# Pooling attention and a routed MLP on one core: 128-token chunks as two 64-column tiles, two attention accumulators, four shared PSUM banks, and half as many comparisons per score

## The chip, the cores and the metric

One core of a Trainium2 chip runs the whole program. The metric is the device time of one execution in microseconds (us), lower is better. The engines of the core are named as in the profile: PE (TensorE, with its weight loads listed apart as PEld), DVE (VectorE), ACT (ScalarE), POOL (GpSimd) and SP (SyncE, which here only issues DMAs).

## The reference

Inputs q, k and v have the shape (8 batches, 8 heads, 576 tokens, 64), all float32. Keys and values are averaged over groups of 8 tokens, so each head has 72 of each.

```python
k_p = k.reshape(B, H, Sp, pool, D).mean(axis=3)
v_p = v.reshape(B, H, Sp, pool, D).mean(axis=3)
scores = scale * np.matmul(q, k_p.transpose(0, 1, 3, 2))
attn = np.exp(scores - max); attn = attn / (np.sum(attn) + 1e-09)
x = np.matmul(attn, v_p)                     # (B, S, H*D) after a transpose
scores = np.einsum('bsd,d->bs', x, w_gate)   # one number per token
top_idx = np.argpartition(-scores[b], capacity)[:capacity]    # 128 of 576
h = np.maximum(x[b, top_idx] @ w1, 0.0)      # 512 -> 1024
out[b, top_idx] = x[b, top_idx] + sigmoid(scores[b, top_idx])[:, None] * (h @ w2)
```

All other rows of `out` are `x`.

## The kernel before

`direct_path` computes the softmax without subtracting the maximum and writes a flag if a sum of exponentials left a safe range; `general_path`, which the change does not touch, would then compute everything again. With these inputs it is not entered.

Attention goes by units and chunks. A batch has 3 units of 192 tokens (`u`) and 6 chunks of 96 tokens (`a`). `q_trans` (L204, DVE) transposes the queries of a unit. `scores` (L209 to L222) makes its scores with 16 float32 matmuls on four row tiles of 32 rows (two heads to a tile pair; 72 key columns as weights, 192 queries streamed), all into `pS`, four PSUM banks with one buffer, and one ACT instruction (L220) takes the exponential of all 1536 columns into `et`, where it writes with a stride. `attend` (L226) runs, per chunk, 8 matmuls, one per head: 96 columns of `et` are the weights, and 66 columns of pooled values `vp` are streamed: 64 values, a column of 8s for the sum, a column of the gate product. The result `pA` is two banks with one buffer. `norm` (L236) reads it: ACT copies the sums (L244, adding eps) and the gate sums (L245), DVE takes the reciprocal (L247) and multiplies (L248) into `xs`. Every float32 matmul appears as two records in the trace, a transpose by a matmul as one.

Pooling adds up raw rows on POOL: `pool_k` (L169, L170) and twice `pool_v` (L186 to L190) per batch, and DVE rearranges the keys (`k_trans`, L175, L179) and reduces the gate product (`gate_v`, L194).

The routed MLP of a batch follows its attention. `score` sums the gate column, `row_bcast` spreads all 576 scores along the free axis (6 transposes, two ACT copies), and `count` compares every score with every other: per chunk one comparison "at least" with the chunks ahead (L305), one "greater" with its own and those behind (L307), and one for ties (L309). `one_hot` and `gather` make a list of 128 rows, an indirect DMA on POOL's queue reads them back from `out` (L331), `x_trans` transposes them, `hidden` runs 8 blocks of 4 matmuls (128 columns each), `finish` 8 matmuls of 512 columns into `pF`, one DVE instruction (L373) adds the residual, and a second indirect DMA (L374) scatters the rows.

Each engine executes in program order, and that order is written out by hand in the loop over `a` (L440 to L452): jobs of slot 0, `attend` and `norm` of chunk `a`, slot 1, `scores` of the next unit (after even `a`) and `q_trans` of the one after it, slots 2 and 3. `at` puts the jobs into slots: the MLP of batch b starts `hidden` at chunk 6(b+1)+8, 14 chunks after the first chunk of the batch, one block per slot, in between the attention of later batches. Loads are issued from SP two batches ahead (the first values and all stores of `xs` from ACT's queue). PSUM is full: 4 banks `pS`, 2 `pA`, 1 `pM` (all small MLP products), 1 `pF`.

Of the kernel before, what the change touches and what calls it, by code (L numbers as in the profile page):

```python
# [7 lines left out]
FT = mybir.dt.float32  # L8
# [40 lines left out]
def direct_path(ctx, tc, q, k, v, moe_w_gate, moe_w1, moe_w2, moe_capacity, out, flag):  # L49
# [7 lines left out]

    nc = tc.nc
# [6 lines left out]
    C = 96  # L65
    NC = S // C
    CT = C // G
    NTH = NC // 2
    N3 = 2 * C
# [8 lines left out]
    assert 2 <= cap <= 128 and DM == 512 and D == 64 and H == 8 and S == 576 and F == 1024  # L78
    NU = B * NTH
    NCH = B * NC  # L80
# [5 lines left out]
    psum = ctx.enter_context(tc.tile_pool(name="psum", bufs=1, space=bass.MemoryType.PSUM))  # L86
# [14 lines left out]
    def load_v(b, g, eng):  # L101
        x = work.tile([SP, HG, POOLW, D], FT, name="vraw", bufs=3)
        VR[b, g] = x
        src = v[b, HG * g : HG * (g + 1)].rearrange("h (p t) d -> p h (t d)", t=POOLW)
        for lo, hi in ((0, 64), (64, SP)):
            eng.dma_start(out=x[lo:hi].rearrange("p h t d -> p h (t d)"), in_=src[lo:hi])

    load_k(0)
    load_v(0, 0, nc.scalar)
    load_q(0)  # L110
    load_v(0, 1, nc.scalar)
# [3 lines left out]
    wg = const.tile([SP, H, D], FT)  # L115
    nc.scalar.dma_start(out=wg.rearrange("p h d -> p (h d)"),
                        in_=bass.AP(tensor=moe_w_gate.tensor, offset=moe_w_gate.offset, ap=[[0, SP], [1, DM]]))
    eps = const.tile([C, 1], FT)
    nc.vector.memset(eps, 1e-9 * POOLW)
    diff = const.tile([128, 128], FT)  # L120
    nc.gpsimd.iota(diff, pattern=[[1, 128]], base=0, channel_multiplier=-1,
                   allow_small_or_imprecise_dtypes=True)
    slots = const.tile([C, cap], FT)
    nc.gpsimd.iota(slots, pattern=[[1, cap]], base=0, channel_multiplier=0,
                   allow_small_or_imprecise_dtypes=True)
    part = const.tile([C, 1], FT)
    nc.gpsimd.iota(part, pattern=[[0, 1]], base=0, channel_multiplier=1, allow_small_or_imprecise_dtypes=True)
    chunk0 = const.tile([C, NC], FT)
    nc.gpsimd.iota(chunk0, pattern=[[1, NC]], base=0, channel_multiplier=0, allow_small_or_imprecise_dtypes=True)
    vps = []  # L130
    for i in range(2):
        t = const.tile([SP, H, E], FT, name=f"vp{i}")
        nc.gpsimd.memset(t[:, :, D : D + 1], float(POOLW))
        vps.append(t)
    ident = const.tile([128, 128], FT)
    before = const.tile([C, C], FT)
    ones = const.tile([C, 1], FT)
    zall = const.tile([C, B, NC, H], FT)
    cmp = const.tile([C, S], BF)
# [4 lines left out]
    def constants():  # L144
        nc.vector.tensor_scalar(ident, diff, 0.0, None, op0=OP.is_equal)
        nc.vector.tensor_scalar(before, diff[:C, :C], 0.0, None, op0=OP.is_lt)
        nc.vector.memset(ones, 1.0)

        hi = const.tile([C, 1], FT, name="hi")
        stepped = const.tile([C, CT], FT, name="stepped")  # L150
        for t in range(CT):
            nc.vector.tensor_scalar(stepped[:, t : t + 1], part, float(G * (t + 1)), None, op0=OP.is_ge)
        nc.vector.tensor_reduce(out=hi, in_=stepped, axis=AX.X, op=OP.add)
        lo = const.tile([C, 1], FT, name="lo")
        nc.vector.scalar_tensor_tensor(lo, hi, -float(G), part, op0=OP.mult, op1=OP.add)
        nc.vector.tensor_scalar(lo, lo, float(NC), None, op0=OP.mult)
        nc.vector.tensor_scalar(hi, hi, float(NC * G), None, op0=OP.mult)
        for a in auxb:
            nc.vector.tensor_scalar(a[:, :, 0], chunk0, lo, None, op0=OP.add)
            nc.vector.tensor_scalar(a[:, :, 1], chunk0, 0.0, hi, op0=OP.mult, op1=OP.add)  # L160
# [11 lines left out]
    def k_trans(b):  # L172
# [4 lines left out]
        KT[b] = work.tile([128, 2, 2, SP], FT, name="kt")  # L177
        x = half.rearrange("p j c r -> p (j c r)").rearrange("p (n two) -> p n two", two=2)
        nc.vector.tensor_tensor(out=KT[b].rearrange("p j s n -> p (j s n)"), in0=x[:, :, 0], in1=x[:, :, 1],  # L179
                                op=OP.add)  # L180
# [17 lines left out]
    QT, ET, XS, SS, RZ = {}, {}, {}, {}, {}  # L198

    def q_trans(u):  # L200

        b, th = divmod(u, NTH)
        QT[u] = work.tile([128, 2, 2, CT, 32], FT, name="qt")
        nc.vector.transpose(  # L204
            out=QT[u].rearrange("p cc j t c -> p t (cc j) c"),
            in_=QR[b].rearrange("p (t c) d -> p t (c d)", c=NC)[:, :, 2 * D * th : 2 * D * (th + 1)].rearrange(
                "p t (a e) -> p t a e", e=32))

    def scores(u):  # L209
        b = u // NTH  # L210
        p = psum.tile([SP, 4, 4, 128], FT, name="pS")
        for s in range(2):
            for j in range(2):
                for i in range(4):
                    r = slice(32 * i, 32 * i + 32)
                    nc.tensor.matmul(p[:, i, 2 * s : 2 * s + 2, 0:C], KT[b][r, j, s, :],  # L216
                                     QT[u][r, :, j, :, G * s : G * s + G],
                                     start=(j == 0), stop=(j == 1))
# [601 lines left out]
```

## Time and profile before

| | |
|---|---|
| three runs | 365.93 us median (361.97 to 368.25) |
| the profiled execution | 366.8 us, of which the span of the trace is 364.9 us |
| busy share of the span | PE 75%, PEld 59%, DVE 49%, POOL 37%, ACT 29% |
| chain that ended last, by engine | PE 44%, DVE 22%, DMA 16%, ACT 6%, issue 5%, POOL 4% |
| mean granted clock of TensorE | 0.865 of full speed |

The profiled execution is a single one, 0.9 us above the median. The chain of work that ended last is followed back from the last instruction through whatever released each step; a line's share of it is the time it set, unlike its busy time. Busy time of PE is modelled by the profiler and records overlap, so a count of records times the distance at which blocks follow each other is a better price than the length of one record. The level of TensorE's clock is 1.2 or 2.4 GHz; a granted clock in between is a mean over a stretch.

### The profile page before, as it was taken

How to read it: one execution, taken by the hardware profiler on the slowest of the kernel's cores; microseconds unless marked ns; L12 is line 12 of the kernel's file. 1: busy time of each engine (PE TensorE's matmuls, PEld its weight loads, DVE VectorE, ACT ScalarE, POOL GpSimd, SP SyncE). 2: the span in 40 equal slices, each digit the busy share in tenths (PEclk: the TensorE clock that was granted, in tenths of full speed). 3: DMA queues.
4: the chain of work that ended last, by engine and by line, in shares of the span. 5: the costliest groups of instructions: out<-in, count | busy, mean ns of one | idle time of the engine just before them, and what ended most of it. 6: DMA issues, size and time to landing. Idle time of an engine off the chain costs nothing.

```text
span 364.9 us, 5869 instructions
## 1 busy us (share of the span) xinstructions
PE 275.2 (75%) x2306; PEld 216.3 (59%) x2306; DVE 177.9 (49%) x524; ACT 104.9 (29%) x169; POOL 134.5 (37%) x156
## 2 busy tenths in 40 slices
PE   0303777788658988969778989698879889989890
PEld 0203666576637875767557755686668669556650
DVE  3249244158423752594429723946294627563001
ACT  0310333422240444324314441432343244110100
POOL 1177501950359015660647064805390210121101
PEclk9999766655565998988999998969996999999996
DMA  7932999961781178306661686031121113210101
GB/s 272 268 58 54 372 353 304 321 140 44 208 249 50 44 195 247 94 15 151 224 158 31 141 295 142 0 110 46 38 65 43 46 29 93 66 60 11 48 0 39
DMA packets 12952, 46.75 MB, mean 128 GB/s; under 512 B 1324, under 2 KB 1324, under 8 KB 10868
## 3 DMA queue, kind: packets, MB, share of 16 engines
q1 hardware_dynamic: 8240, 31.33, 29.4%
q10 hardware_dynamic: 3396, 10.77, 10.0%
q0 software_dynamic: 1280, 4.20, 4.2%
q8 instruction: 20, 0.33, 0.4%
q14 instruction: 16, 0.13, 0.1%
HBM read 34.75 MB, written 11.53 MB: 127 GB/s over the span
## 4 chain that ended last, share of the span: by engine, by line
PE 44%; DVE 22%; DMA 16%; ACT 6%; issue 5%; POOL 4%; ACTq 1%; DVEq 0%; SPq 0%; POOLq 0%
PE pA L232 14%; PE pM L358 10%; PE pS L216 8%; DMA xr<-out_dram,idx 8%; PE pF L368 8%; DMA vraw<-in_v_dram 7%; DVE xs L248 4%; ACT et L220 4%; DVE cmp L309 3%; POOL kraw L169 2%; DVE cmp L305 2%; DVE qt L204 2%; DVE cmp L307 2%; DVE oh L316 2%; DVE kh L175 2%
## 5 line engine op out<-in xcount | busy, mean ns | idle before, releaser
L232 PE MATMUL pA<-vp,et 72*96 72x66 f32 x768 | 90.8, 281 | 47.7 <-DVE vp L194 24.6
L232 PEld LDWEIGHTS pA<-vp,et 72*96 72x96 f32 x768 | 86.3, 195 | 59.0 <-issue 28.5
L220 ACT ACTIVATE et<-pS 72x1536 f32<-72x1536 f32 x24 | 70.7, 2947 | 61.9 <-PE pS L216 61.9
L358 PE MATMUL pM<-xg,w 128*128 128x128 f32 x512 | 71.3, 292 | 2.8 <-ACT xg L348 1.5
L358 PEld LDWEIGHTS pM<-xg,w 128*128 128x128 f32 x512 | 65.0, 203 | 8.7 <-issue 5.0
L368 PE MATMUL pF<-w,ht 128*128 128x512 f32 x128 | 65.2, 632 | 0.0
L247 DVE RECIPROCAL rz<-zall 96x8 f32<-96x8 f32 x48 | 9.5, 198 | 113.9 <-ACT zall L244 112.4
L216 PE MATMUL pS<-qt,kt 32*72 32x192 f32 x768 | 52.4, 428 | 12.0 <-DVE qt L204 12.0
L216 PEld LDWEIGHTS pS<-qt,kt 32*72 32x72 f32 x768 | 36.5, 184 | 19.4 <-DVE qt L204 12.0
L281 POOL CAST auxb<-sc 96x6 bf16<-96x6 f32 x8 | 1.6, 199 | 121.0 <-DVE sc L277 105.0
L186 POOL TENSOR_TENSOR vraw<-vraw 72x1024 f32<-72x1024 f32 x15 | 35.5, 2368 | 19.7 <-DMA vraw<-in_v_dram 19.6
L244 ACT ACTIVATE zall<-pA,eps 96x8 f32<-96x8 f32 x48 | 12.2, 254 | 93.8 <-PE pA L232 93.8
L248 DVE TENSOR_TENSOR xs<-pA,rz 96x512 f32<-96x512 f32 x48 | 33.0, 687 | 6.7 <-DVE rz L247 0.9
L368 PEld LDWEIGHTS pF<-w,ht 128*128 128x128 f32 x128 | 22.9, 200 | 17.9 <-issue 17.9
L307 DVE TENSOR_SCALAR_CACHE_REDUCE cmp<-sr,sc 96x576 bf16<-96x576 f32 (+5 forms) x48 | 26.6, 554 | 0.0
L204 DVE STREAM_TRANSPOSE qt<-qraw 128x768 f32<-128x768 f32 x24 | 23.2, 966 | 0.9 <-DMA qraw<-in_q_dram 0.9
L374 POOL DMA_INDIRECT out_dram<-y,idx x8 | 8.5, 1064 | 40.1 <-DVE y L373 22.0
L309 DVE SCALAR_TENSOR_TENSOR cmp<-sr,sc,before 96x96 bf16<-96x96 f32 x48 | 21.9, 456 | 0.3
L373 DVE SCALAR_TENSOR_TENSOR y<-pF,g,xr 128x512 f32<-128x512 f32 x8 | 6.0, 750 | 29.5 <-PE pF L368 29.5
L305 DVE TENSOR_SCALAR_CACHE_REDUCE cmp<-sr,sc 96x96 bf16<-96x96 f32 (+4 forms) x40 | 20.0, 499 | 0.7
L187 POOL TENSOR_TENSOR vraw<-vraw 72x512 f32<-72x512 f32 x15 | 19.1, 1277 | 1.2
L361 ACT ACTIVATE ht<-pM 128x512 f32<-128x512 f32 x16 | 9.6, 597 | 33.6 <-PE pM L358 33.6
(68 smaller groups left out, 182.4 us busy)
## 6 DMA issues: line engine op xcount, KB each, us to landing
kraw<-in_k_dram SPq DMA_DIRECT2D x8, 1152.0 KB
qraw<-in_q_dram SPq DMA_DIRECT2D x8, 1152.0 KB, 6.7
out_dram<-xs ACTq DMA_DIRECT2D x24, 384.0 KB, 3.0
vraw<-in_v_dram SPq DMA_DIRECT2D x14, 512.0 KB, 9.0
w<-in_moe_w_dram SPq DMA_DIRECT2D x2, 2048.0 KB, 27.3
vraw<-in_v_dram ACTq DMA_DIRECT2D x2, 512.0 KB, 19.9
vraw<-in_v_dram SPq DMA_DIRECT2D x14, 64.0 KB
wg<-in_moe_w_gate_dram ACTq DMA_DIRECT2D x1, 144.0 KB
```

Of the source, the lines that this page charges most:

```text
L186: eng.tensor_tensor(out=x[:, :, 0:4, :], in0=x[:, :, 0:4, :], in1=x[:, :, 4:8, :], op=OP.add)
L187: eng.tensor_tensor(out=x[:, :, 0:2, :], in0=x[:, :, 0:2, :], in1=x[:, :, 2:4, :], op=OP.add)
L204: nc.vector.transpose(out=QT[u].rearrange("p cc j t c -> p t (cc j) c"), in_=QR[b].rearrange("p (t c) d -> p t (c d)", c=NC)[:, :, 2 * D * ...
L216: nc.tensor.matmul(p[:, i, 2 * s : 2 * s + 2, 0:C], KT[b][r, j, s, :], QT[u][r, :, j, :, G * s : G * s + G], start=(j == 0), stop=(j == 1))
L220: nc.scalar.activation(ET[u].rearrange("p n g t -> p n t g"), p.rearrange("p i n x -> p (i n) x")[:, :, 0:C].rearrange("p n (t g) -> p n t ...
L232: nc.tensor.matmul(p[:, g, E * n : E * n + E], ET[u][:, 2 * h + cc].rearrange("p g t -> p (g t)"), VP[b][:, h, :], start=True, stop=True)
L248: nc.vector.tensor_tensor(out=XS[b][:, c, :].rearrange("p (g n d) -> p g n d", g=2, d=D), in0=o[:, :, :, 0:D], in1=rz.rearrange("p (g n on ...
L305: nc.vector.tensor_scalar(cmp[:, 0 : c * C], row[:, 0 : c * C], s, None, op0=OP.is_ge, op1=OP.add, accum_out=CN[b][:, c, 0:1])
L307: nc.vector.tensor_scalar(cmp[:, c * C : S], row[:, c * C : S], s, None, op0=OP.is_gt, op1=OP.add, accum_out=CN[b][:, c, 1:2])
L309: nc.vector.scalar_tensor_tensor(cmp[:, 0:C], row[:, c * C : c * C + C], s, before, op0=OP.is_equal, op1=OP.mult, accum_out=CN[b][:, c, 2:3])
L358: nc.tensor.matmul(p[:, f % 4, :], w1[:, d, 128 * f : 128 * f + 128], XG[b][:, d, :], start=(d == 0), stop=(d == DB - 1))
L368: nc.tensor.matmul(p, HT[b][:, f, :], w2[:, f, :], start=(f == 0), stop=(f == FB - 1))
```

## The change

Tokens are taken in tiles of 64 (`TL`), 9 to a batch; a unit is three tiles (still 192 tokens), and a chunk two tiles, 128 tokens, so that two batches share 9 chunks. In `attend` each of the 8 heads has two matmuls with 64 weight columns each; one writes PSUM partitions 0 to 63, the other 64 to 127 of the same bank. `pA` gets two buffers. The four banks that scores use are now single tiles `bank0` to `bank3`, which all MLP products share; each bank has its own exponential, and `et` is written densely. Pooled values and keys are spread over 128 partitions with zeros between (an extra one carries eps), so score matmuls have 128 weight columns. `norm` leaves ACT: DVE takes the reciprocal from PSUM and forms the gate score.

`count` makes one "at least" comparison per chunk, with the chunks up to its own, times a mask, with the sum along the row; `one_hot` gets the other half of each count as 15 matmuls of the comparison matrices with a column of ones. `hidden` runs in parts of 3, 3 and 2 blocks, `finish` in three column slices (176, 176, 160), each scaled on ACT and added on POOL. Stores and all loads of values move to SP's queue. Value loads get four fixed buffers. The slots are rearranged: `hidden` of batch b starts in unit 3(b+1)+3, and scores run two units ahead at the start, one later.

```diff
+    vraws = [const.tile([128, HG, POOLW, D], FT, name=f"vraw{i}") for i in range(4)]
+    for i, t in enumerate(vraws):
+        (nc.vector, nc.gpsimd)[i % 2].memset(t, 0.0)
...
+        nc.sync.dma_start(out=x[0:128:2], in_=src[0:64])
+        nc.sync.dma_start(out=x[1:128:16], in_=src[64:SP])
...
+    first = const.tile([C, 1], FT)
+    nc.vector.memset(first, 1.0)
+    nc.scalar.activation(first, first, AF.Exp)
...
+        nc.vector.tensor_reduce(out=y[:, :, 0:128:2], in_=x[:, :, 0:64, :], axis=AX.X, op=OP.add)
+        nc.vector.tensor_reduce(out=y[:, :, 1:128:16], in_=x[:, :, 64:SP, :], axis=AX.X, op=OP.add)
...
+        for s in tiles_of(b, th):
+            x = QR[b][:, s, :].rearrange("p t (j e) -> p t j e", e=32)
+            m = x.shape[1]
+            nc.vector.transpose(out=QT[u][:, :, n : n + m, :].rearrange("p j t c -> p t j c"), in_=x)
...
+        p = [bank(i, [128, 2, TS * TL]) for i in range(4)]
...
+                    nc.tensor.matmul(p[i][:, s, :], KT[b][r, j, s, :], QT[u][r, j, :, G * s : G * s + G],
                                      start=(j == 0), stop=(j == 1))
+        ET[u] = [work.tile([128, 2, TS * TL], FT, name=f"et{i}", bufs=3) for i in range(4)]
+        for i in range(4):
+            nc.scalar.activation(ET[u][i], p[i], AF.Exp, scale=exp_scale)
...
+        PA[a] = psum.tile([C, 2, 512], FT, name="pA")
...
+            for t in range(2):
+                u, i = divmod(2 * a + t, TS)
+                nc.tensor.matmul(PA[a][TL * t : TL * t + TL, g, E * n : E * n + E],
+                                 ET[u][h // 2][:, h % 2, TL * i : TL * i + TL], VP[u // NTH][:, h, :],
+                                 start=True, stop=True)
...
+        nc.vector.reciprocal(rz, o[:, :, :, D])
...
+        nc.vector.tensor_tensor(out=SS[a // NT][:, a % NT, :].rearrange("p (g n) -> p g n", g=2),
+                                in0=o[:, :, :, D + 1], in1=rz, op=OP.mult)
...
+        for i, cs in enumerate((range(0, NC - 1), range(NC - 1, NC))):
+            p = bank(i, [C, len(cs), C])
...
+        for c in range(NC):
+            nc.vector.scalar_tensor_tensor(GE[b][c], SR[b][:, 0 : c + 1, :], scs[b % 2][:, c : c + 1],
+                                           before[:, NC - 1 - c : NC, :], op0=OP.is_ge, op1=OP.mult,
+                                           accum_out=CN[b][:, c : c + 1])
...
+        p = bank(2, [C, NC])
+        for c in range(NC):
+            for i in range(c, NC):
+                nc.tensor.matmul(p[:, c : c + 1], GE[b][i][:, c, :], ones, start=(i == c), stop=(i == NC - 1))
...
+        fs = range(FB)[3 * part : 3 * part + 3]
+        p = bank(nb, [128, len(fs), cap])
...
+        c = slice(176 * part, min(176 * part + 176, DM))
+        p = bank(nb, [cap, c.stop - c.start])
+        for f in range(FB):
+            nc.tensor.matmul(p, HT[b][:, f, :], w2[:, f, c], start=(f == 0), stop=(f == FB - 1))
+        nc.scalar.activation(Y[b][:, c], p, AF.Copy, scale=g)
+        nc.gpsimd.tensor_tensor(out=Y[b][:, c], in0=Y[b][:, c], in1=XR[b][:, c], op=OP.add)
...
+        for n, f in enumerate((row_bcast, count, one_hot, gather, gate, x_trans)):
+            du, slot = ((0, 1), (0, 2), (0, 6), (1, 4), (1, 6), (2, 5))[n] if b == B - 1 else (
+                (0, 3), (0, 7), (1, 3), (1, 7), (2, 2), (2, 7))[n]
+            at(w + du, slot, f, b)
+        at(w + 3, 3, hidden, b, 0, 0)
+        at(w + 3, 5, hidden, b, 1, 1)
+        at(w + 4, 3, hidden, b, 2, 0)
+        at(w + 4, 5, finish, b, 0, 1)
+        at(w + 5, 5, finish, b, 1, 2)
+        at(w + 5, 6, finish, b, 2, 3)
...
+            at(u, 1, pool_k, b + 1, nc.gpsimd)
+            at(u, 7, pool_v, b + 1, 0, nc.gpsimd)
+            at(u + 1, 3, k_trans, b + 1)
+            at(u + 1, 7, pool_v, b + 1, 1, nc.gpsimd)
...
+    load_k(1)
+    load_v(1, 0)
+    load_v(1, 1)
+    load_q(1)
...
+    constants()
     pool_k(0, nc.vector)
     pool_v(0, 0, nc.gpsimd)
     k_trans(0)
     q_trans(0)
     scores(0)
+    q_trans(1)
+    scores(1)
+    eights()
+    gate_v(0, 0)
     pool_v(0, 1, nc.vector)
     gate_v(0, 1)
...
+    for u in range(NU + 6):
+        run(u, 0)
+        mine = chunks.get(u, ())
+        for a in mine[0:1]:
+            attend(a)
+            norm(a)
+        run(u, 1)
+        if 0 < u < NU - 1:
             scores(u + 1)
+        run(u, 2)
+        for a in mine[1:]:
+            attend(a)
+            norm(a)
+        if u + 2 < NU:
+            q_trans(u + 2)
+        for slot in range(3, 8):
+            run(u, slot)
```

A unit `u` has one chunk when it is even and two when it is odd; `w` is 3(b+1).

## Rows read from the trace of the kernel before

**Rows 1.** The page's first part: busy time and instructions of each engine.
```profile
PE 275.2 (75%) x2306; PEld 216.3 (59%) x2306; DVE 177.9 (49%) x524; ACT 104.9 (29%) x169; POOL 134.5 (37%) x156
```
**Rows 2.** Chain of waits, 30 to 63 us: start us, us, what. One unit.
```profile
42.48 2.83 PE pA L232 x16
45.30 2.82 PE pS L216 x32
...
48.21 2.93 ACT et L220
...
51.52 0.70 DVE xs L248
...
52.27 2.83 PE pA L232 x16
```
**Rows 3.** Stretches: from:to, us, busy us (records) PE, PEld, DVE, ACT, POOL, granted clock, DMA.
```profile
33.00:111.00 78.00, 55.73 (x466) 46.89 (x467) 34.41 (x105) 25.05 (x40) 30.53 (x34) 0.64 0.79 240
111.00:148.60 37.60, 34.86 (x288) 27.20 (x289) 19.05 (x62) 13.01 (x21) 14.08 (x17) 0.84 0.48 134
...
261.60:298.80 37.20, 32.42 (x292) 25.94 (x290) 21.56 (x63) 13.03 (x21) 13.78 (x17) 0.91 0.16 47
```
**Rows 4.** Chain of waits, 111 to 365 us: blocks of records, in order of time.
```profile
120.65 1.33 PE pA L232 x16
121.98 1.84 PE pM L358 x16
...
126.10 1.47 PE pS L216 x32
127.57 1.09 PE pM L358 x8
...
180.97 7.21 DMA xr<-out_dram,idx
...
316.35 0.30 PE pM L323 x6
...
319.26 0.45 PE pM L293 x3
...
322.39 0.64 PE pM L346 x4
...
349.69 6.03 PE pF L368 x14
355.74 0.75 DVE y L373
```
**Rows 5.** Timeline of PEld, 301 to 303 us: the weight loads of one unit's scores.
```profile
301.29 1.19 PEld L216 LDWEIGHTS pS<-qt,kt 32*72 32x72 f32 x32
```
**Rows 6.** Groups by line and shape: operation, shapes, count, busy us, mean ns, idle before.
```profile
L232 PE MATMUL pA<-vp,et 72*96 72x66 f32 x768 | 90.8, 281 | 47.7 <-DVE vp L194 24.6 <-DVE xs L248 20.6 <-DVE ss L275 2.5
L186 POOL TENSOR_TENSOR vraw<-vraw 72x1024 f32<-72x1024 f32 x15 | 35.5, 2368 | 19.7 <-DMA vraw<-in_v_dram 19.6
L361 ACT ACTIVATE ht<-pM 128x512 f32<-128x512 f32 x16 | 9.6, 597 | 33.6 <-PE pM L358 33.6
L295 ACT COPY sr<-pM 96x288 f32<-96x288 f32 x16 | 6.7, 418 | 8.0 <-PE pM L293 8.0
```
**Rows 7.** Timeline, 148 to 189 us: POOL and DVE side by side, then DVE's instruction again.
```profile
155.63 2.34 POOL L186 TENSOR_TENSOR vraw<-vraw 72x1024 f32<-72x1024 f32 x1
...
155.98 2.11 DVE L309 SCALAR_TENSOR_TENSOR cmp<-sr,sc,before 96x96 bf16<-96x96 f32 x1
...
161.15 0.31 DVE L309 SCALAR_TENSOR_TENSOR cmp<-sr,sc,before 96x96 bf16<-96x96 f32 x1
```
**Rows 8.** Timeline, 0 to 36 us: the start.
```profile
2.27 31.39 SPq L106 DMA_DIRECT2D vraw<-in_v_dram  x4
...
16.72 2.35 POOL L186 TENSOR_TENSOR vraw<-vraw 72x1024 f32<-72x1024 f32 x1 [15.17 <-DMA vraw<-in_v_dram]
...
32.96 2.80 PE L232 MATMUL pA<-vp,et 72*96 72x66 f32 x16 [18.09 <-DVE vp L194]
```

More of the change, by code (lines that the diff above doesn't have):

```diff
@@ L123, in direct_path @@
[L123 to L134, printed above, removed]
@@ new lines, in direct_path @@
+    vps = [const.tile([128, H, E], FT, name=f"vp{i}") for i in range(2)]
+    kts = [const.tile([128, 2, 2, 128], FT, name=f"kt{i}") for i in range(2)]
+    for t in kts + vps:
+        nc.gpsimd.memset(t, 0.0)
+    slots = counted("slots", [C, NC, cap], [[C, NC], [1, cap]], 1 - NC * C, 1)
+    before = const.tile([C, NC, C], FT)
+    nc.gpsimd.memset(before[:, 0 : NC - 1, :], 1.0)
+    scs = [const.tile([C, NC], FT, name=f"sc{i}") for i in range(2)]
+    nc.gpsimd.memset(scs[0][TL:C, NC - 1 : NC], -3e38)
@@ L145, in constants @@
         nc.vector.tensor_scalar(ident, diff, 0.0, None, op0=OP.is_equal)
-        nc.vector.tensor_scalar(before, diff[:C, :C], 0.0, None, op0=OP.is_lt)
+        nc.vector.tensor_scalar(before[:, NC - 1, :], diff, 0.0, None, op0=OP.is_lt)
         nc.vector.memset(ones, 1.0)
[L149 to L160, printed above, removed]
+        nc.vector.memset(one32, 1.0)
@@ L256, in direct_path @@
+    SR, CN, GE, OH, XR, GV, XG, HT, Y = ({} for _ in range(9))
     store, scat, gath = {}, {}, {}
@@ L319, in gather @@
     def gather(b):
-        p = psum.tile([cap, 5], FT, name="pM")
+        p = bank(2, [cap, 5])
         for c in range(NC):
@@ L343, in x_trans @@
     def x_trans(b):
-        p = psum.tile([128, DB, cap], FT, name="pM")
+        p = bank(0, [128, DB, cap])
         for d in range(DB):
@@ L348, in x_trans, with hidden @@
         nc.scalar.copy(out=XG[b], in_=p)
-    def hidden(b, f):
-        if f == 0:
+    def hidden(b, part, nb):
+        if part == 0:
             HT[b] = work.tile([128, FB, cap], FT, name="ht")
-        if f % 4 == 0:
-            PH[b] = psum.tile([128, 4, cap], FT, name="pM")
-        p = PH[b]
-        for d in range(DB):
-            nc.tensor.matmul(p[:, f % 4, :], w1[:, d, 128 * f : 128 * f + 128], XG[b][:, d, :],
-                             start=(d == 0), stop=(d == DB - 1))
-        if f % 4 == 3:
-            nc.scalar.activation(HT[b][:, f - 3 : f + 1, :], p, AF.Relu)
@@ new lines, in hidden, with finish @@
+        p = bank(nb, [128, len(fs), cap])
+        for n, f in enumerate(fs):
+            for d in range(DB):
+                nc.tensor.matmul(p[:, n, :], w1[:, d, 128 * f : 128 * f + 128], XG[b][:, d, :],
+                                 start=(d == 0), stop=(d == DB - 1))
+        nc.scalar.activation(HT[b][:, fs[0] : fs[-1] + 1, :], p, AF.Relu)
+    def finish(b, part, nb):
+        idx, g = GV[b]
+        if part == 0:
+            Y[b] = work.tile([cap, DM], FT, name="y")
+        c = slice(176 * part, min(176 * part + 176, DM))
[4 more added lines that the diff above has]
+        nc.gpsimd.tensor_tensor(out=Y[b][:, c], in0=Y[b][:, c], in1=XR[b][:, c], op=OP.add)
+        if part == 2:
+            i = nc.gpsimd.indirect_dma_start(
+                out=out_rows, out_offset=bass.IndirectOffsetOnAxis(ap=idx[:, :1], axis=0), in_=Y[b], in_offset=None)
+            others(i, b, (store, scat, gath))
+            scat[b] = [i]
```

321 lines of the change are left out of this document (150 added, 171 removed).

## Prediction

> **What bounds the kernel now.** I read the busy shares first. TensorE is the busiest engine, at 75% of the span [rows 1], but an average over stages settles nothing, so the stretches come next. Three stages show: nothing but attention until 111 us, then five batches in which attention and MLP interleave, then two MLPs alone.
>
> In the first stage TensorE is busy 55.73 of 78 us, at a mean granted clock of 0.64 [rows 3]. The chain of waits says why that is no TensorE bound: a unit goes round in 9.79 us (42.48 to 52.27), as attend 2.83, scores 2.82, exponential 2.93, division 0.70 [rows 2]. Two properties make it a ring. `pA` has one buffer, so the next attend waits for the division; and the division's inputs come from ACT, which in program order first does the exponential of the next unit. Blocks here last twice as long as later: attend 2.83 against 1.33, scores 2.82 against 1.47 [rows 2, 4]. That is the lower of the two clock levels.
>
> In the middle stage five batches take 187.8 us (111.0 to 298.8), 37.6 each, of which TensorE is busy 32.42 in the last, at a granted clock of 0.91 [rows 3]. Block distances at the high level give its bare work per batch: attend 6 x 1.33 = 8.0; scores 3 x 1.47 = 4.4; hidden, 64 records at 1.84/16 = 0.115, 7.4; finish, 16 at 6.03/14 = 0.43, 6.9; 6 broadcasts at 0.15, 6 small products at 0.05 and 4 transposes at 0.16, 1.8 [rows 4]. The sum is 28.5, so 9.1 us per batch are waits and low clock. The ring of the first stage still exists here, and the read-back of the gathered rows takes 7.21 us [rows 4].
>
> **The change, part by part.**
>
> *Attend.* A chunk of 128 tokens has 32 records instead of 16, and a batch 4.5 chunks instead of 6. No row shows column tiles, so both bounds are worked out. Hidden streams 128 columns and loads 128 in 0.115 us per record, attend loads 96 and streams 66 in 0.083 [rows 4]: 0.9 ns per column, whichever of the two is longer, the other hidden. With 64 loaded and 66 streamed a record costs 0.059. If the two tiles go one after the other, a chunk takes 32 x 0.059 = 1.88 us; if side by side, 0.94. The nearest row is scores, which run four row tiles: 32 records of 192 streamed columns would take 5.5 us in turn and take 1.47 [rows 4], 0.11 above a quarter. I take side by side with that surcharge, 1.05 us per chunk, 4.7 per batch, and keep 8.5 as the other end.
>
> *Scores.* The streamed columns stay, the loaded ones grow from 72 to 128. All 32 loads now lie within 1.19 us [rows 5]; in proportion 2.1, if they are the limit, 1.47 if not. I take 1.6, since the loads overlap across row tiles; 4.8 per batch.
>
> *Mode changes.* Attend becomes a tiled block between scores (row tiles) and MLP (none). Where the trace has such a change, the 8 records of hidden behind scores take 1.09 instead of 0.92 [rows 4]: 0.17. Per batch there are 10.5 changes instead of 6; at 0.17 that is 0.8 more. Here a rule speaks against the change: the Trainium skill, TensorEngine Tiling (Array Packing), Key Properties, says that changing the tiling mode drains the engine, while changing the tile within a mode does not. If such a drain cost a whole record's 0.28 us [rows 6] each time, the sum would grow by 1.3 instead of 0.8 per batch, 3 us over the kernel; the trace's 0.17 is what I use.
>
> *MLP.* Hidden stays 7.4. Finish loads its weights three times as often, but 176 columns streamed at 0.9 ns still cover 128 loaded: 48 records, 7.4. Broadcasts, 5 at 0.16, 0.8. Column sums are new: 15 small products like gather's, 0.05 each [rows 4], 0.75. Gather and transposes 0.9. With attend, scores and mode changes TensorE's bare work is 27.5 us per batch.
>
> *ACT* loses the sums and copies of `norm`, and the stores' issue. Rows of 512 and 288 dense columns, 0.597 and 0.418 [rows 6], give 0.19 plus 0.8 ns per column, so an exponential of 384 costs 0.5, four 2.0, instead of 2.93. TensorE hides all of it: scores are a unit ahead. Without cover it would be 2 us per unit.
>
> *DVE* gets one small product more per chunk but counts in five instructions instead of 17. Rows of 96 and 512 columns, 0.31 and 0.75 [rows 4, 7], give 0.2 plus 1.06 ns per column: 128 to 640 columns, 3.1 us plus five reads of the sum. DVE was busy 21.56 us in a batch [rows 3]; at or below that it lies under TensorE's 27.5. `q_trans` and `k_trans` in two pieces cost some tenths and hide there too. POOL has 134.5/8 = 16.8 us per batch [rows 1] and gets three additions, 176 columns at 2.368/1024 each [rows 6], 1.2 more: hidden.
>
> *Counting under POOL.* A masked comparison of 96 columns took 2.11 us while POOL ran a pooling step, and 0.31 alone [rows 7]. The new count is five such instructions with two inputs, and a batch's first `pool_v` is queued right behind it. The least extra is nothing; the most is one POOL step before each, about the 4.7 us of one `pool_v` (2048 columns at 2.3 ns). The Trainium skill, SBUF — State Buffer, Who interferes with whom, has it so: two inputs from SBUF contend with POOL reading SBUF, one input does not. If by that rule the whole 4.7 fell on each count with no cover, the sum would be 6 x 3.7 = 22 us longer, near rival 2. The row bears it out in kind, not in how often. Between count and the column sums, TensorE has hidden, attend and scores of some 7 us to do, so I charge 1 us of wait.
>
> *Waits that remain,* per batch: the broadcast now shares a bank with hidden and waits for its Relu (0.6 [rows 6]), the next hidden part waits for the broadcast's copy (0.9), count 1, read-back 1. Together 3.5. The ring of [rows 2] is gone: with two `pA` buffers an attend waits for the division of the chunk before last. A batch then takes 27.5 + 3.5 = 31 us against 37.6.
>
> *Queue of SP.* Stores wait there for `xs`, with the loads of two batches later behind them. In the old start SP is held 31.39 us by value loads that wait for a buffer [rows 8]; four buffers end that. A store waits at most a unit, and loads have two batches: nothing is charged.
>
> *Start.* Values are ready for POOL at 16.72, the first attend runs at 32.96 [rows 8]. In the new order POOL pools one half (4.7), DVE reduces it (0.4), pools the other (2048 columns at 1.06, 2.2) and reduces that: 25 us; 33 if POOL holds DVE up as before.
>
> *First two batches,* six units. POOL's pooling, 5824 columns per batch at 2.3 ns, is 4.5 us per unit; TensorE needs 1.5 x 1.05 + 1.6 = 3.2 at the high clock level and 6.4 at the low one. I take 5.7, bounds 4.5 and the old 9.79. That is 34 us.
>
> *Tail* after the last unit: two hidden and two finish 29.6, broadcast, sums, gather, transposes 2.4, two Relus and copies 1.2, a wait for read-back 3, and from the last finish to the span's end 364.9 - 355.7 = 9.2 [rows 4] plus some tenths: 46.
>
> *Sum:* 25 + 34 + 6 x 31 + 46 = 291, plus the 1.9 us that the profiled execution has outside its span (366.8 - 364.9): 293. That execution lies 0.9 above the median of the runs, which I neglect.
>
> **The rivals.**
>
> 1. *Tiles in turn.* Attend 8.5 instead of 4.7: 34.8 per batch, 1 us more at start and 1 in the tail: 293 + 6 x 3.8 + 2 = 318. For it: no row shows column tiles. Against: row tiles overlap.
> 2. *The waits stay.* Sharing banks and counting under POOL cost what the ring cost, 9.1 instead of 3.5: 293 + 6 x 5.6 = 327. For it: [rows 7] and the in-order wait of the column sums for the last comparison. Against: 7 us of work in between.
> 3. *The first six units keep their pace* of 9.79, the clock low and POOL or DMA the limit: 293 + 25 = 318. Against: nothing of the old ring is left.
> 4. *Slower: column tiles that do not pipeline.* If each record took its own length, 0.281 [rows 6], a chunk would take 9.0 us, a batch 67: 293 + 6 x 36 = 509. It decides from 365.9 on, when a batch takes 31 + 73/6 = 43 us, attend 3.8 us per chunk, 0.119 per record: twice the price in turn, which is what tiles in turn at the low clock level would cost. Against: in the middle stage the long MLP blocks lifted the granted clock from 0.64 to 0.84 and more [rows 3].
>
> **How the numbers follow.** Forecast (up to 310) 0.52; rival 1 0.17, rival 2 0.12, rival 3 0.07, rivals 1 and 2 together (350) 0.05, rival 4 0.07. The forecast's own range comes from its bounds: 268 (no waits but 1 us, units of 5.2, start 23) to 310. The range of 8 in 10 reaches to 330, past the first three rivals. Between runs the old kernel differs by 2%, which is about what a measurement can tell from no change: faster by over 2% 0.88, within 2% 0.04, slower 0.08.
>
> **What would show it.** Right: attend blocks of 32 records about 1.05 us apart at the high level; first attend near 25 us; hidden of batch 0 starting near 60; batches 31 us apart; waits of attend for the division gone from the list. Wrong: attend blocks near 1.9 (rival 1); waits of TensorE for the last comparison or for ACT's copies above 5 us per batch (rival 2); units near 9 us before 60 (rival 3); a granted clock near 0.5 between 60 and 240 us (rival 4).

## The result and the profile after

The changed kernel takes 293.1 us (median of four runs, 291.6 to 295.5) against 366.4 before: a ratio of 0.804, 95% interval 0.793 to 0.814. The forecast was 293, range 268 to 330. Medians here are over all executions; ratios leave out those that are over 1.5% slower than the fastest of their kernel. The profiled execution has a span of 292.5 us. That the total fits to the microsecond is luck: two stages were longer than their terms, two shorter. The page's first part answers [rows 1]:

```profile
PE 222.7 (76%) x3050; PEld 205.6 (70%) x3050; DVE 147.9 (51%) x367; ACT 72.9 (25%) x178; POOL 156.9 (54%) x191
```

TensorE's share is what it was; its busy time fell by 52 us. The stretches of the kernel after (columns as in [rows 3]) show where the time lies. The first row ends where the second half of the first attend runs (its first half has run at 20.13, then TensorE waits for the second half of the values), the second with the first attend of unit 6, the third about where unit 9 begins; the last begins after unit 23.

```profile
0.00:27.90 27.90, 6.29 (x82) 5.18 (x82) 24.16 (x40) 4.76 (x10) 22.55 (x30) 0.93 0.93 323
27.90:70.60 42.70, 24.60 (x463) 21.36 (x463) 28.13 (x66) 9.61 (x24) 23.54 (x24) 0.78 0.77 277
70.60:104.30 33.70, 29.93 (x369) 27.66 (x369) 13.73 (x41) 8.60 (x22) 17.78 (x21) 0.88 0.58 188
104.30:252.40 148.10, 131.38 (x1887) 121.47 (x1887) 76.91 (x203) 42.75 (x106) 82.72 (x100) 1.00 0.39 123
252.40:292.50 40.10, 30.46 (x256) 29.90 (x255) 4.99 (x19) 7.17 (x18) 10.30 (x18) 0.93 0.11 37
```

The same for the stretch from the first attend of unit 6 to the end of the last attend, first in the kernel before, then after:

```profile
94.60:312.70 218.10, 185.99 (x1668) 148.82 (x1669) 119.03 (x364) 74.30 (x123) 91.17 (x103) 0.89 0.40 112
70.60:247.20 176.60, 156.10 (x2219) 144.15 (x2219) 89.12 (x237) 50.56 (x125) 99.02 (x118) 0.98 0.43 137
```

This stretch gives 41 of the 72 us between the two spans, the first six units 19 (61.6, from 33.0 to 94.6, to 42.7), the start 5, the end 7. In it TensorE's busy time falls by 30 us, and its idle time by 12.

From 104.3 to 252.4 us TensorE is busy 89% of the time at a granted clock of 1.00: this stage is bound by TensorE's own work. Its busy share was no lower before, 34.86 of 37.6 and 32.42 of 37.2 us, but at a granted clock of 0.84 and 0.91 [rows 3]. The chain of waits has the block prices, as [rows 4] has those of before: 32 records of attend in 1.09 us, scores 1.59 (1.51 elsewhere), 15 column sums 0.35, a third of finish 2.50, hidden 7.14.

```profile
115.95 1.09 PE pA L289 x32
117.04 1.59 PE bank L277 x32
...
121.22 0.35 PE bank L385 x15
121.58 2.50 PE bank L442 x16
...
270.00 7.14 PE bank L430 x64
```

The list of waits of the kernel after (who waited for whom: us in total, times, longest) names what is left. Attend's wait for the division, 20.6 us before [rows 6], has no line any more. The last line below, scores behind a reciprocal, is not that wait: scores don't read the division, and in both places (31.2 and 37.9 us) DVE had just finished transposing queries or keys for them. The new waits come from sharing: DVE behind POOL, and blocks that use one bank after each other.

```profile
DVE g L413 <- POOL g L412: 41.0, 8, 6.5
...
PE pA L289 <- DVE vp L241: 12.0, 6, 7.1
...
PE bank L430 <- ACT sr L369: 5.7, 7, 1.1
PE bank L442 <- ACT et L281: 5.0, 5, 1.4
PE bank L385 <- DVE ge L376: 4.3, 3, 1.7
PE bank L418 <- DMA xr<-out_dram,idx: 4.3, 1, 4.3
...
PE bank L430 <- ACT et L281: 3.7, 6, 0.6
PE bank L368 <- ACT ht L432: 3.5, 6, 0.6
PE bank L277 <- DVE rzall L298: 3.4, 2, 3.0
```

### The profile page after: what moved, and what is told of

The parts are those of the page before. It is cut to its first block, busy times and chain, and to the rows that moved or that the text cites. A ratio compares the mean times of both kernels' runs of the same rounds, so it can differ in the third digit from the quotient of the medians.

```text
span 292.5 us, 7287 instructions
## 1 busy us (share of the span) xinstructions
PE 222.7 (76%) x3050; PEld 205.6 (70%) x3050; DVE 147.9 (51%) x367; ACT 72.9 (25%) x178; POOL 156.9 (54%) x191
## 4 chain that ended last, share of the span: by engine, by line
PE 50%; POOL 17%; DVE 12%; issue 10%; ACT 4%; DMA 3%; POOLq 0%; ACTq 0%
PE bank L430 16%; PE bank L442 14%; PE bank L277 8%; PE pA L289 8%; POOL vraw L233 5%; DMA vraw<-in_v_dram 3%; DVE ge L376 3%; POOL vraw L234 3%; DVE qt L267 2%; ACT et L281 2%; POOL kraw L215 2%; POOL vp L235 2%; POOL vraw L237 1%; ACT sr L369 1%; PE bank L368 1%
## 5 line engine op out<-in xcount | busy, mean ns | idle before, releaser
L430 PE MATMUL bank<-xg,w 128*128 128x128 f32 x512 | 64.2, 284 | 9.4 <-ACT sr L369 5.7
L430 PEld LDWEIGHTS bank<-xg,w 128*128 128x128 f32 x512 | 60.4, 196 | 13.5 <-ACT sr L369 7.4
L442 PE MATMUL bank<-w,ht 128*128 128x176 f32 (+1 forms) x384 | 59.2, 311 | 5.0 <-ACT et L281 5.0
L281 ACT ACTIVATE et<-bank 128x384 f32<-128x384 f32 x96 | 39.3, 496 | 92.6 <-PE bank L277 92.6
L442 PEld LDWEIGHTS bank<-w,ht 128*128 128x128 f32 x384 | 55.8, 190 | 6.3 <-ACT et L281 6.2
L277 PE MATMUL bank<-qt,kt 32*128 32x192 f32 x768 | 43.8, 364 | 18.3 <-DVE qt L267 14.4
L289 PE MATMUL pA<-vp,et 128*64 128x66 f32 x1152 | 46.6, 234 | 12.4 <-DVE vp L241 12.0
L289 PEld LDWEIGHTS pA<-vp,et 128*64 128x64 f32 x1152 | 40.8, 146 | 18.8 <-DVE vp L241 7.2
L376 DVE SCALAR_TENSOR_TENSOR ge<-sr,sc,before 128x128 bf16<-128x128 f32 (+4 forms) x40 | 37.8, 1003 | 30.1 <-ACT sr L369 30.1
L277 PEld LDWEIGHTS bank<-qt,kt 32*128 32x128 f32 x768 | 35.9, 205 | 20.9 <-issue 17.6
```

The source lines that it names most:

```text
L277: nc.tensor.matmul(p[i][:, s, :], KT[b][r, j, s, :], QT[u][r, j, :, G * s : G * s + G], start=(j == 0), stop=(j == 1))
L281: nc.scalar.activation(ET[u][i], p[i], AF.Exp, scale=exp_scale)
L289: nc.tensor.matmul(PA[a][TL * t : TL * t + TL, g, E * n : E * n + E], ET[u][h // 2][:, h % 2, TL * i : TL * i + TL], VP[u // NTH][:, h, :] ...
L376: nc.vector.scalar_tensor_tensor(GE[b][c], SR[b][:, 0 : c + 1, :], scs[b % 2][:, c : c + 1], before[:, NC - 1 - c : NC, :], op0=OP.is_ge, ...
L430: nc.tensor.matmul(p[:, n, :], w1[:, d, 128 * f : 128 * f + 128], XG[b][:, d, :], start=(d == 0), stop=(d == DB - 1))
L442: nc.tensor.matmul(p, HT[b][:, f, :], w2[:, f, c], start=(f == 0), stop=(f == FB - 1))
```

## The experiments

Ratios are to the kernel before, executed beside each changed one on the same chip. Medians are compared with 293.1, or with each other, across chips, so differences of a few us are rough. A median is of four executions, with one profiled among them; it is of ten for the division on DVE, of seven for the exponential by bank and of six for the last kernel.

### The two tiles of a chunk in turn

```diff
-        for h in range(H):
-            for t in range(2):
+        for t in range(2):
+            for h in range(H):
```

> The changed kernel with one difference: within a chunk all 8 heads of the first 64-column tile come first, then the 8 heads of the second, so that neighbouring matmuls use the same tile; the instructions are the same. Theory (neighbouring column tiles run side by side, 1.09 us per chunk in the changed kernel): a chunk now takes the price in turn, about 1.88 us at the high clock level, 36 x 0.8 = 28 us more, of which waits that shrink give a little back: 310 to 322 us. Rival (the tiles do not overlap, and the blocks are short for another reason, such as the smaller weight loads): the block stays at 1.09 us and the time at 293.

311.6 us, ratio 0.861 (0.854 to 0.869). The same instructions in another order cost 18.5 us. Chain of waits of this kernel:

```profile
162.30 1.84 PE pA L289 x32
164.14 1.59 PE bank L277 x32
```

A chunk takes 1.84 us instead of 1.09: side by side is real, and the price in turn is the 1.88 of the prediction. In the middle a batch grew by 2.3 us (32.6 between hidden blocks against 30.3), not by 4.5 x 0.75 = 3.4. TensorE's waits between unit 6 and the last attend fell from 20.3 to 16.9 us, which is about half of that difference over six batches; the other half is not accounted for.

### One accumulator

```diff
-        PA[a] = psum.tile([C, 2, 512], FT, name="pA")
+        PA[a] = psum.tile([C, 2, 512], FT, name="pA", bufs=1)
```

> The changed kernel with one buffer for pA instead of two; two banks of PSUM lie idle. Theory A (what opened the ring is the division's move off ACT; between two attend blocks there are almost always 1.5 us of scores or an MLP block on TensorE, which cover the 1.1 us of the division): 293 to 303 us. Theory B (the second buffer is what opened the ring): every chunk waits some 1.2 us for its predecessor's division, 36 x 1.2 = 43 us more: about 336 us.

297.7 us, ratio 0.823 (0.815 to 0.830): 4.6 us more by the medians, 1.4 between the profiled executions. Theory B falls. Scores or an MLP block stand between most attends, and the second buffer only pays where DVE is late. In the list of waits of this kernel that is 4 of 36 attends:

```profile
PE pA L289 <- DVE ss L309: 4.1, 4, 1.2
```

The first six units take 42.8 us, against 42.7 with two buffers.

### Three comparisons per chunk

```diff
-            nc.vector.scalar_tensor_tensor(GE[b][c], SR[b][:, 0 : c + 1, :], ..., op0=OP.is_ge, op1=OP.mult, ...)
+            if c: nc.vector.tensor_scalar(cmp[:, 0 : c * C], row[:, 0 : c * C], s, None, op0=OP.is_ge, op1=OP.add, ...)
+            nc.vector.tensor_scalar(cmp[:, c * C : NC * C], row[:, c * C : NC * C], s, None, op0=OP.is_gt, op1=OP.add, ...)
+            nc.vector.scalar_tensor_tensor(cmp[:, 0:C], row[:, c * C : c * C + C], s, before[:, NC - 1, :], op0=OP.is_equal, ...)
```

> The changed kernel with the old way of counting: per chunk of 128 an 'at least' comparison with the chunks ahead, a 'greater' one with its own and those behind and one for ties, 14 instructions instead of 5, and no column sums on TensorE. By the rows of before (0.2 us plus 1.04 ns per column, and 0.08 for each read of the sum) DVE then has 8.0 us of counting per batch where the changed kernel shows 5.1. Theory (DVE is covered by TensorE, except in the first units and at the end): 293 to 300 us. Rival (TensorE waits for the count in every batch): 2.9 us more in each of 8 batches, about 316 us.

299.0 us, ratio 0.826 (0.819 to 0.834): 5.9 us more, at the upper end of the theory's range. But the place is not the theory's: of the 3.8 us between the profiled spans 0.9 lie in the first six units and 2.8 behind them, where DVE was to be covered. Groups of this kernel's DVE, all forms together (count | busy, mean ns):

```profile
L382 DVE TENSOR_SCALAR_CACHE_REDUCE cmp<-sr,sc 128x640 bf16<-128x640 f32 (+4 forms) x40 | 24.4, 609 | 31.2 <-ACT sr L370 31.2
L384 DVE SCALAR_TENSOR_TENSOR cmp<-sr,sc,before 128x128 bf16<-128x128 f32 x40 | 19.0, 474 | 0.3
```

The one-input comparisons, 384 columns in the mean, take 0.609, what 0.2 + 384 x 1.04 ns gives; the two-input one with the mask takes 0.474 in the mean where it takes 0.35 alone. Only the second kind is held up by POOL: of the 40, the 26 that meet no pooling take 0.346 to 0.353, the 14 that run beside it 0.363 to 1.373, while one-input comparisons of one width differ by some 2% at most, beside pooling or not. DVE is busy 17 us more than in the changed kernel (164.9 against 147.9), of which a third reaches the end.

### The old kernel with the division on DVE

```diff
-        nc.scalar.activation(z.rearrange(...), o[:, :, :, D], AF.Identity, bias=eps)
-        nc.scalar.copy(out=SS[b][:, c, :].rearrange(...), in_=o[:, :, :, D + 1])
+        nc.vector.tensor_scalar(z.rearrange(...), o[:, :, :, D], eps, None, op0=OP.add)
+        nc.vector.tensor_copy(SS[b][:, c, :].rearrange(...), o[:, :, :, D + 1])
```

> The kernel before with one difference: the two small ACT instructions of the division (sums plus eps, gate sums) are on DVE, so that the division no longer waits behind the exponential of the next unit. Theory (ACT's program order closes the ring of the first 111 us): a unit there goes from 9.8 us to the time of its TensorE blocks with the division between them, 5 to 8 us, and the middle batches from 37.6 to 34 to 36: 320 to 345 us. Rival (the single pA buffer and the low clock keep the pace): 360 to 370 us.

360.7 us, ratio 0.991 (0.984 to 0.999). The theory falls. The chain of waits of one unit, and a line of the next:

```profile
50.59 2.80 PE pA L232 x16
53.38 2.78 PE pS L216 x32
56.16 2.77 PE pA L232 x16
...
59.45 0.69 DVE xs L248
...
60.28 2.80 PE pA L232 x16
...
65.99 2.93 ACT et L220
```

In this unit the exponential is out of the chain, and it still takes 9.69 us (50.59 to 60.28): TensorE's three blocks at the lower clock level are 8.35 of it, and the division, which the next attend still waits for because of the one accumulator, is the rest. In the next unit the exponential is back in the chain. The first six units take 59.9 us (32.7 to 92.6) against 61.6: ACT's order hid a second bound of nearly the same length.

### Old kernel, operands of full height, alone and with the division on DVE

```diff
-        KT[b] = work.tile([128, 2, 2, SP], FT, name="kt")
+        KT[b] = kts[b % 2]          # 128 wide, columns 72 to 127 zero
...
-        p = psum.tile([SP, 4, 4, 128], FT, name="pS")
+        p = psum.tile([128, 4, 4, 128], FT, name="pS")
```

> The kernel before with keys padded by zeros to 128 weight columns and pooled values and exponentials to 128 partitions, as the changed kernel has them; everything else is old. In the first 111 us of the kernel before, TensorE's blocks ran at the lower clock level nearly throughout (mean granted clock 0.64); in the changed kernel the stage behind the first attend has 0.78. Theory (the operands' height is what differs): the granted clock of the first stage rises and its units shorten, total 340 to 355 us. Rival (order and waits decide the clock): first stage as before, 360 to 372 us.

> Both single steps in the old kernel: zero-padded operands and the division on DVE. With the division on DVE alone a unit of the first stage still took 9.7 us, as TensorE's three blocks at the lower clock level are 8.4 of it. Theory (the clock is what remains, and the operands raise it): blocks halve, units of 5 to 7 us, 335 to 350 us. Rival: as the division on DVE alone, 357 to 365 us.

357.2 us, ratio 0.971 (0.958 to 0.983), and 352.4, ratio 0.959 (0.944 to 0.974). Both times lie between theory and rival. Neither opens the first stage: granted clock 0.66 and 0.71, first MLP block at 116 and 109.5 us, against 114.4 before. The first kernel's gain lies behind it, where its granted clock is 0.97 (112.6 to 300 us), against 0.91 in the same stretch before. That the height of the operands raised the clock is not shown: these are single executions, and the kernel before had mean clocks between 0.816 and 0.959 over whole executions.

### Old kernel, division on DVE and exponential by bank; and all three parts

Both kernels also have the division on DVE (edit above), the second the operands of full height besides. The new edit is:

```diff
-        p = psum.tile([SP, 4, 4, 128], FT, name="pS")
+        p = [psum.tile([SP, 4, 128], FT, name=f"pS{i}") for i in range(4)]
...
-        nc.scalar.activation(ET[u].rearrange("p n g t -> p n t g"), p.rearrange(...), AF.Exp, scale=exp_scale)
+        for i in range(4):
+            nc.scalar.activation(ET[u][i].rearrange("p n g t -> p n t g"), p[i][...], AF.Exp, scale=exp_scale)
```

> The old kernel with the division on DVE and, as a second difference, the exponential of a unit in four pieces, one for each bank of scores (strided writes stay), so that attend starts behind the first piece and the next scores behind the first bank. In the old order attend needs the exponential of scores that ended one chunk before, 2.9 us that TensorE has 1.3 us of work for at the high clock level. Theory (this wait is what keeps TensorE idle and its clock low in the first stage, and the division on DVE alone left it): units of the first stage go from 9.7 to 5 to 7 us with the higher clock level, 320 to 340 us. Rival (the single pA buffer is enough to keep the pace): 350 to 360 us, as the division on DVE alone.

> The old kernel with three parts of the change together: zero-padded operands of full height, the division on DVE, the exponential in four pieces by bank. Left out are the 128-token chunks in two tiles, the second accumulator, the shared banks, the new count and the new order of jobs. Operands and division alone gave 352 us, division and exponential alone 359. Theory (the three together free the first stage, as each alone leaves one of low clock and waits): 325 to 342 us, the first MLP block before 100 us instead of 114. Rival (chunks and order are needed): 345 to 355 us, the first MLP block behind 104 us.

359.3 us, ratio 0.986 (0.982 to 0.991), and 351.7, ratio 0.964 (0.957 to 0.970). Both times lie in the rival's range; that the one accumulator is what keeps the pace, as the first rival says, is not shown by that. The first stage of the kernel with all three parts, in the stretch that answers the first row of [rows 3]:

```profile
32.70:110.00 77.30, 57.32 (x493) 52.80 (x494) 39.15 (x137) 22.43 (x34) 36.84 (x38) 0.69 0.81 247
```

TensorE is busy longer than in the kernel before and still at a low mean clock. Operands, division and exponential by bank together bring 13 us of the 73. The rest comes from the other parts: the 128-token chunks in tiles, dense exponentials, shared banks, the new count, the queues, the new order of jobs. Taken out singly from the changed kernel, tiles side by side, second accumulator and count cost 18.5, 4.6 and 5.9 us. If the parts simply add up, an estimate, some 30 of the 73 us belong to no part that was tried.

### Values pooled earlier

```diff
-            at(u + 1, 7, pool_v, b + 1, 1, nc.gpsimd)
+            at(u + 1, 1, pool_v, b + 1, 1, nc.gpsimd)
```

> The changed kernel with the second half of a batch's value pooling one place earlier in POOL's order: at the start of the unit (slot 1) instead of behind the gather of the other batch (slot 7). Theory (POOL stands idle 7 to 9 us in front of the gather, waiting for the list of rows, and the pooling behind it is late for the first attend of the next batch: waits of TensorE for it sum up to 12 us in the changed kernel): these waits go, 7.1 us of them lie before the first attend and stay, so 5 us less, 286 to 290 us. Rival (they only move to the read-back, which is as late): 293 us.

296.0 us, ratio 0.812 (0.803 to 0.820), not to be told from the changed kernel's. Nothing was gained: TensorE's waits for pooled values fell from 12.0 to 5.1 us, those for the read-back rose from 4.3 to 6.7, as the rival has it. The line of the count in this kernel (min/median/max ns) shows another thing that went against it: more of the count runs beside POOL's pooling, and its median comparison takes 1162 ns, against 880 in the changed kernel.

```profile
L376 DVE SCALAR_TENSOR_TENSOR ge<-sr,sc,before x40: 351/1162/2975, 49.4 to 257.7; 128x128 bf16<-128x128 f32 x8, 128x256 bf16<-128x256 f32 x8, 128x384 bf16<-128x384 f32 x8, 128x512 bf16<-128x512 f32 x8
```

### Other bank numbers

```diff
-            p = bank(i, [C, len(cs), C])
+            p = bank(2 + i, [C, len(cs), C])
...
-        p = bank(0, [128, DB, cap])
+        p = bank(3, [128, DB, cap])
...
-        at(w + 5, 5, finish, b, 1, 2)
-        at(w + 5, 6, finish, b, 2, 3)
+        at(w + 5, 5, finish, b, 1, 0)
+        at(w + 5, 6, finish, b, 2, 1)
```

> The changed kernel with other numbers for the shared banks: the broadcast goes to banks 2 and 3 instead of 0 and 1, the last two slices of finish to 0 and 1 instead of 2 and 3, the transposed rows to 3 instead of 0; order and work stay. Theory (per batch TensorE waits 0.6 us for a Relu, 0.8 for the broadcast's copy and about 0.9 for the third exponential, because neighbours in its order share a bank): about 2.3 us less in each of some 7 batches: 275 to 283 us. Rival (it waits for the same engines a moment later, above all for the count): 290 to 294 us.

281.3 us, ratio 0.772 (0.764 to 0.780): 11.8 us less for other bank numbers. The waits for the broadcast's copy and for the Relu ahead of it are gone, a batch takes 28.7 us instead of 30.3 in the middle.

### The start on POOL

```diff
-    pool_v(0, 1, nc.vector)
+    pool_v(0, 1, nc.gpsimd)
```

> The changed kernel with the other bank numbers and, besides, the second half of the first batch's values pooled on POOL, behind the first half and ahead of the next batch's keys, instead of on DVE. In the changed kernel DVE takes 8.9 us for it next to POOL, where the same columns take POOL 5.1 us. Theory (the start is 4 us shorter and the rest follows): the first attend at about 24 us instead of 28, 275 to 279 us. Rival (POOL's pooling of the next batch is 5 us later and the first units wait for that): 280 to 283 us.

This kernel has the other banks too. 283.5 us, ratio 0.780 (0.774 to 0.785), beside 0.772 (0.764 to 0.780) without this edit: nothing gained, as the rival has it, if anything a loss. The second half of the first attend comes at 23.6 us instead of 27.9, yet that of unit 6 at 72.7 (70.6 in the changed kernel), behind 4.5 us of waiting for pooled values. The 4 us were given back within six units.

### The gate on DVE

```diff
-        nc.gpsimd.tensor_scalar(g, g, 1.0, None, op0=OP.add)
+        nc.vector.tensor_scalar(g, g, 1.0, None, op0=OP.add)
```

> The changed kernel with the other bank numbers and one more difference: the addition of 1 in the gate is on DVE instead of POOL. In the changed kernel DVE waits 41 us in 8 places for this 0.2 us instruction, which stands behind 5 us of value pooling in POOL's order, and divisions and query transposes stand behind it on DVE. Theory (a part of this reaches TensorE, which waits 13 us for pooled values and divisions in the kernel with other banks): 270 to 278 us. Rival (DVE has the time): 280 to 282 us.

277.5 us, ratio 0.762 (0.758 to 0.765), on top of the other banks: 3.8 us less than with those alone. The interval just touches the one with the other banks alone (0.764 to 0.780); the slowest execution here took 277.8, the fastest there 280.0. DVE's wait ahead of the gate's reciprocal falls from 41.9 us, for POOL, to 20.6, now for ACT in front of the addition. This is the fastest kernel of the study, 5% below the changed one by a few bank numbers and one engine's name. In its list of waits, TensorE's for pooled values:

```profile
PE pA L289 <- DVE vp L241: 5.2, 2, 5.1
```

With the other banks alone these were 13.4 us in 7 places: the late `gate_v` stood on DVE behind a reciprocal that waited for POOL's 0.2 us addition, and that addition behind a pooling of 5 us. The read-back took some of it back (TensorE waits 5.8 us for it instead of 3.4), and of the 3.4 us between the two profiled spans 2.4 lie in the first six units.

## Why the prediction was right, and where it was not

**Attend, scores, MLP: right.** Attend 1.09 us per chunk, forecast 1.05; scores 1.51 to 1.59, forecast 1.6; hidden 7.1, forecast 7.4; finish 7.1 to 7.3, forecast 7.4. Column sums cost 0.35 per batch, half of the forecast. Per batch of 30.3 us TensorE's busy share of 89% is 26.9 us, forecast 27.5. The choice between the ends for the column tiles, by likeness to row tiles, is what carried this; the tiles in turn show the other end was priced right too.

**The waits of the middle: right in sum, by luck.** 3.4 us per batch are waits, forecast 3.5, but they are not the same waits. From unit 6 to the last attend of the kernel after:

```profile
PE bank L430 <- ACT sr L369: 5.0, 6, 1.1
PE bank L442 <- ACT et L281: 5.0, 5, 1.4
PE pA L289 <- DVE vp L241: 5.0, 5, 1.9
PE bank L430 <- ACT et L281: 3.7, 6, 0.6
PE bank L368 <- ACT ht L432: 3.5, 6, 0.6
```

The broadcast's copy (0.8 per batch, forecast 0.9) and the Relu (0.6, forecast 0.6) came as forecast. Count and read-back, 1 each in the sum, hold TensorE up nowhere here. In their place stand two waits that the sum did not have: 1.4 per batch for exponentials out of banks that hidden and finish want next, and 0.5 for pooled values (of the 5.0, 1.9 fall at the very start and belong to the first six units).

**Mode changes: right in size.** Behind an attend block 24 records of hidden take 2.89 us (168.51 to 171.40), while 64 in a row take 7.14 [chain above], 2.68 for 24: 0.21 for a change, forecast 0.17.

```profile
168.51 2.89 PE bank L430 x24
...
260.51 1.89 PE bank L430 x16
```

Not all of it is the mode: the second line is hidden behind the column sums, which have no tiles, and there 16 records take 1.89 instead of 1.79, 0.1 more. The Trainium skill, TensorEngine Tiling (Array Packing), Key Properties, says that a change of mode drains the engine. The trace agrees that there is a price, and it lies below a record's length of 0.28.

**Counting: price right, charge in the wrong place.** Timeline of DVE and POOL in the kernel after, first with POOL at work, then in the last batch without it:

```profile
48.28 1.67 DVE L376 SCALAR_TENSOR_TENSOR ge<-sr,sc,before 128x256 bf16<-128x256 f32 x1
...
49.63 2.53 POOL L233 TENSOR_TENSOR vraw<-vraw 128x1024 f32<-128x1024 f32 x1
...
49.89 2.69 DVE L376 SCALAR_TENSOR_TENSOR ge<-sr,sc,before 128x384 bf16<-128x384 f32 x1
...
254.79 0.48 DVE L376 SCALAR_TENSOR_TENSOR ge<-sr,sc,before 128x256 bf16<-128x256 f32 x1
...
255.19 0.62 DVE L376 SCALAR_TENSOR_TENSOR ge<-sr,sc,before 128x384 bf16<-128x384 f32 x1
```

Alone the five take 0.35 to 0.89, together 3.1, as worked out. Over all batches they take 37.8/8 = 4.7. The Trainium skill, SBUF — State Buffer, Who interferes with whom, has a DVE instruction with two SBUF inputs contend with POOL's reads, and one with a single input not, outside the modes in which DVE uses both its port pairs. This and the three comparisons bear it out. In the middle the 7 us of cover hold, and the charge of 1 us per batch did not arise; in the first six units, where there is no MLP to cover with, the count of batch 0 takes 47.6 to 55.5 us and its column sums hold TensorE up for some 5.6 of them (1.4 of that is put down to the exponential in the bank that they write).

**The start: 27.9, forecast 25.** The term that failed is the second half of the values on DVE, 2.2 us "alone". POOL pooled the next keys and values beside it. Timelines as in [rows 8], one line of the kernel before, then the kernel after:

```profile
24.40 3.62 DVE L187 TENSOR_TENSOR vraw<-vraw 72x512 f32<-72x512 f32 x1
```

```profile
12.77 2.35 POOL L233 TENSOR_TENSOR vraw<-vraw 128x1024 f32<-128x1024 f32 x1 [4.18 <-DMA vraw<-in_v_dram]
...
18.40 3.29 DVE L233 TENSOR_TENSOR vraw<-vraw 128x1024 f32<-128x1024 f32 x1
21.72 1.77 DVE L234 TENSOR_TENSOR vraw<-vraw 128x512 f32<-128x512 f32 x1
23.53 2.45 DVE L235 TENSOR_TENSOR vp<-vraw 128x256 f32<-128x256 f32 x1
26.01 1.37 DVE L237 TENSOR_TENSOR vraw<-vp,wg 128x256 f32<-128x256 f32 x1
```

That is 8.9 us; values reached POOL 4 us earlier than in [rows 8], which hid most of the error. The prediction named the other end, 33 us if POOL holds DVE up as before, and chose this one. The kernel before had the price in its trace: the same four steps took DVE 8.8 us there (23.14 to 32.03), beside POOL.

**The first six units: 42.7 us, forecast 34.** 7.1 us each instead of 5.7, and hidden of batch 0 starts at 76.1, which the prediction had near 60. TensorE is idle for 18.1 us: the count of batch 0 (5.6), its list of rows (2.3), the read-back (4.3), pooled values (1.9) and transposed keys (3.0) each stop it once, and 1.0 in small pieces. The waits that were charged to the middle fall here, without cover. TensorE's clock does not set this stage: it takes 42.9 us at a granted clock of 0.74 with the other banks, 42.7 at 0.78 in the changed kernel and 42.8 at 0.84 with one accumulator.

**The middle and the tail: shorter.** 30.3 us per batch instead of 31, 181.8 instead of 186 in all; the tail 40.1 instead of 46, since the charged 3 us for the last read-back did not arise (finish of the batch before covers it), Relus are covered by parts, and from the last finish to the end it is 8.4 us instead of 9.2.

**The reading of the first stage: wrong in its cause.** The prediction put its pace to a ring through one accumulator and ACT's order. The division on DVE took ACT out of the ring and nearly nothing changed, since TensorE's blocks at the lower clock level and the division behind them took as long. One accumulator leaves the changed kernel's stage at 42.8 us. The measured 7.1 us per unit lie between the forecast's bounds, 4.5 and the old 9.79; what its 5.7 was chosen from, POOL's 4.5 and TensorE's 6.4 at the low level, did not rest on the ring. The low clock alone is not the cause either: the kernel before took 366.3 us in an execution with a mean clock of 0.816 and 361.2 in one with 0.959, of which no trace was kept. What frees the stage stays open: it needs more than operands, division and exponential by bank, and neither the second accumulator nor tiles side by side (the kernel with tiles in turn has 44.6 us there). Left are the shorter list of blocks (9 chunks instead of 12), the dense exponentials, four buffers for values and the order of jobs; they weren't tried one by one.

**Queue of SP: nothing charged, nothing seen.** SP stands behind stores for up to 14 us (119.8 to 134.0) with loads queued behind them, but no wait of TensorE leads to a late load in the kernel after.

## What to carry to other kernels

Where blocks share a few buffers, look at which neighbours in the engine's own order share one: numbers alone were worth 12 us here. A tiny instruction on an engine with long ones is a wait for its readers as long as the long ones: 0.2 us on POOL held DVE for 41 us in 8 places, though moving it shortened the kernel by only some 4. And before a chain of waits is called the cause, sum up the bound engine's own blocks: here a ring through ACT and TensorE at its low clock level had nearly the same length, and removing ACT from the ring left the other. A term that has two prices, alone and beside another engine, takes the one that the trace shows for the same neighbours: the start lost 6.7 us to the choice of the other.

## What the hardware showed that was not expected

TensorE's clock did not follow its busy share. In the old kernel with the exponential by bank, TensorE was busy by its records for 58.8 of 77.0 us (33 to 110) at a mean granted clock of 0.54; in the changed kernel's first units for 24.6 of 42.7 at 0.78. Part of the larger share is the low clock itself, at which attend's and scores' blocks last twice as long [rows 2, 4]. And ACT's exponential depends on how it writes: 384 columns take 0.494 us into a dense tile in the changed kernel, and 0.902 with a stride of six elements in the old kernel's exponential by bank (0.898 in the kernel with all three parts, whose tile has 128 partitions, as the dense one has, so the height is not the reason).
